# Linear attention feeding a gated MLP on one core: S loaded in two transfers, x scaled tile by tile, and a new order table

## The chip, the cores and the metric

The kernel runs on one core of a Trainium2 chip. The metric is the device time of one execution in microseconds (us). Before the change it was 259.46 us, the median of three runs (258.75, 259.46 and 259.86).

## The reference

The program computes a linear attention and puts its result through a normalised, gated MLP, all in fp32:

```python
def phi(x):                                   # per token: 8 x 8 outer product, 64 features
    a = np.einsum('rd,bhsd->bhsr', S1, x)
    b = np.einsum('rd,bhsd->bhsr', S2, x)
    return np.einsum('bhsi,bhsj->bhsij', a, b).reshape(*x.shape[:-1], r * r)
q_p, k_p = phi(q), phi(k)                     # 4 batches, 4 heads, 1088 tokens, head_dim 32
kv = np.einsum('bhsf,bhsd->bhfd', k_p, v);  z = np.sum(k_p, axis=2)
num = np.einsum('bhsf,bhfd->bhsd', q_p, kv)
den = np.einsum('bhsf,bhf->bhs', q_p, z)[..., None] + 1e-06
x = (num / den), as 4352 tokens x 128
xn = x / sqrt(mean(x * x) + 1e-06) * rms_g
out = (silu(xn @ w_gate) * (xn @ w_val)) @ w_out        # 128 -> 1536 -> 128
```

## The kernel before

**Tiling.** The 4352 tokens are cut into eight chunks of 512 and one of 256. For each of the four batches `kside` computes the key features and the product `kv`; for each chunk `qside` computes the query features, the numerators (L627), the denominators (L645/L646, L649), x (L636), the mean squares `ms` (L655), `rstd` on GpSimd (L668), the scaled rows `xn` (L671 on VectorE or L688 on ScalarE), their transposes on TensorE (L675), and the two parts `x_hi` and `x_lo` (L678, L681) of the MLP's input. The MLP goes by slots: one chunk and one of the 12 blocks of 128 of the 1536 hidden columns. A slot is three matmuls each for the gate and the value (L726: high by high, low weight by high, high weight by low), Silu on ScalarE (L735), the product `h` on VectorE (L738), its high part on ScalarE (L753), its low part on VectorE or GpSimd (L756), and three matmuls into `o_ps` (L764). Weights and S arrive as 64-bit words and are turned into fp32 with bit operations (L346 to L362 for the weights, L371 to L389 for S).

**Start.** S is the small matrix (`sw`, 128 rows of 512 bytes, 64 KB). It lands in `s_raw` and becomes `sblk`, which every first-stage matmul (L485 for keys, L550 for queries) takes as an operand. S is one transfer, the first on ScalarE's DMA queue (L392). The first half of chunk 0 of q follows it on that queue (L524); the other half is on SyncE's queue, behind the first piece of the keys (L457). TensorE runs eight warm-up matmuls on a constant (L337) meanwhile.

**Order.** Nothing is scheduled on the chip: the string `ORDER` lists the numbers of all tasks (1286 of them), and the string `ON` says, for each task that could run on more than one engine, which one has it (a for ScalarE, d for VectorE, p for GpSimd). `Plan.follow` walks the list with a cost for each task and gives each a start; `Plan.run` writes the instructions in the order of these starts. A transfer with a `since` is taken to start at that time; one whose `since` is 0 takes the next place on the common DMA clock. Where the plan sees TensorE idle for long, it puts in further warm-up matmuls.

Of the kernel before, what the change touches and what calls it, by code (L numbers as in the profile page):

```python
# [22 lines left out]
P = 128  # L23
# [61 lines left out]
"""  # L85
ON = (
    "aapddadapaaapaddaaaaaappapdadpapdapdadpadpapdapdaddappappadapadddapaddaaaapdddddaadapapdaaaddddaddddddadpdddddpppdpapdda"
    "paaaadpaaadpddppdppddpaaaddaaapppddpddddppaaadpdddpdpddpddddddadadpdddpdppddppdpdpdaappaaddpppppddpdpddadpddapdpdpddpddd"
    "dadpdddppddpa"
# [15 lines left out]
SLATE = 650  # L105
# [156 lines left out]
def attention_then_glu(ctx, tc, kT, v, qT, sw, w, out):  # L262
# [19 lines left out]
    def on_act(n, emit, sbuf=False, against=0):  # L282
        occ = n * 0.835 + (98 if sbuf else 62)
        return Way(occ, occ + 98, emit, against=against)

    def on_dve(n, emit, lock=False, fast=False, against=0):
        occ = n * (0.52 if fast else 1.04) + 70
        return Way(occ, occ + 82, emit, lock or fast, against)
# [99 lines left out]
    def s_join():  # L388
        nc.vector.tensor_tensor(out=sblk.bitcast(U32), in0=s_tmp.bitcast(U32), in1=s_top, op=ALU.bitwise_or)  # L389

    plan.add({"dma": Way(
        ISSUE + SLATE, P * NB * 8 / 320, lambda: nc.scalar.dma_start(out=s_raw.rearrange("p n c -> p (n c)"), in_=sw.bitcast(U32)), since=740  # L392
    )}, (), ["s_raw"])
# [5 lines left out]
    plan.add({"act": on_act(NB, s_abs, True), "dve": on_dve(NB, s_abs_dve, fast=True)}, ["s_raw", "table"], ["s_tmp"])  # L399
    dve(NB, s_side, ["s_raw"], ["s_top"], fast=True)  # L400
    dve(NB, s_low, ["s_raw", "s_top"], ["s_top"], lock=True)
# [116 lines left out]
    def qload(c):  # L518
        n, s0 = CHUNKS[c], STARTS[c]
        q = qs[c] = sb("q", [P, 512], 2)  # L520
        for i, (lo, hi) in enumerate(((0, n // 2), (n // 2, n)) if not c and QHALVES else ((0, n),)):
            eng = nc.sync if c or i else nc.scalar
            load(
                P * (hi - lo) * 4, lambda eng=eng, lo=lo, hi=hi: eng.dma_start(out=q()[:, lo:hi], in_=qT[:, s0 + lo:s0 + hi]), [(q, i)],  # L524
                since=0 if c or i else 1170,
            )

    def qside(c):
# [133 lines left out]
        for u, wd in ((0, 2), (2, 2)) if first else ((0, nt),):  # L662
# [7 lines left out]
            def scaled(us=us, wd=wd):  # L670
                nc.vector.tensor_tensor(out=xn()[:, us], in0=x()[:, us], in1=rstd()[:, us].to_broadcast([P, wd, DM]), op=ALU.mult)  # L671
# [197 lines left out]
```

## Time and profile before

| | before |
|---|---|
| median of three runs | 259.46 us (258.75 to 259.86) |
| the profiled execution's own time | 258.33 us |
| its span, first to last instruction | 256.5 us |
| TensorE busy | 252.0 us, 98% |
| VectorE / ScalarE / GpSimd busy | 168.6 / 153.8 / 90.6 us |
| granted TensorE clock | 1.00 |

The profiled execution took 1.83 us more than its span, which lies outside the first and last instruction, and it is 1.13 us below the median of the three runs. A row of the timeline gives the start in us from the span's start, the duration, the engine (a "q" behind the name is the engine's instruction queue, which issues DMAs), the line, and the tile written and those read; in brackets stands idle time ahead of it and what ended that. PEld is TensorE's weight load, which runs beside its matmuls. A matmul's duration covers its pipeline, so successive matmuls overlap; the spacing of their starts is what each costs.

### The profile page before, as it was taken

What the parts mean: (1) busy time and instruction counts of PE and PEld (TensorE: products, weight loads), DVE (VectorE), ACT (ScalarE), POOL (GpSimd) and SP (SyncE); (2) the same over time, 40 slices, a digit from 0 to 9 for tenths busy, and PEclk for the clock granted to TensorE, in tenths of its full rate; (3) what the DMA queues carried; (4) which work ended last, traced back from release to release, by engine and by line L of the source; (5) the groups of instructions that cost most, each with busy time, mean ns of one, the idle gap of its engine ahead of it and who ended that gap; (6) DMA issues with size and microseconds to landing.
All of it is one profiled execution on the core that took longest, in us unless ns stands there. A gap on an engine that the chain in (4) does not pass through costs nothing.

```text
span 256.5 us, 5598 instructions
## 1 busy us (share of the span) xinstructions
PE 252.0 (98%) x2116; PEld 204.0 (80%) x2116; DVE 168.6 (66%) x390; ACT 153.8 (60%) x339; POOL 90.6 (35%) x92
## 2 busy tenths in 40 slices
PE   7999999999999999999999999999999999999995
PEld 5888777788887787788887888888888887888895
DVE  2998999989866676646464666647644554635643
ACT  3789888647664744575555555455556655554572
POOL 3444222123755412583516503145223714132031
PEclk9999999999999999999999999999999999999999
DMA  7999886064015115061320120001000100100010
GB/s 236 380 382 279 251 236 208 0 158 130 1 59 149 65 47 139 0 185 43 92 75 3 42 78 15 0 1 43 0 0 0 41 4 0 41 0 3 0 42 20
DMA packets 13498, 22.13 MB, mean 86 GB/s; under 512 B 1952, under 2 KB 5024, under 8 KB 13472
## 3 DMA queue, kind: packets, MB, share of 16 engines
q1 hardware_dynamic: 13040, 21.52, 27.0%
q8 instruction: 16, 0.26, 0.4%
q10 hardware_dynamic: 432, 0.26, 0.3%
q14 instruction: 10, 0.08, 0.1%
HBM read 18.69 MB, written 3.08 MB: 85 GB/s over the span
## 4 chain that ended last, share of the span: by engine, by line
PE 95%; ACT 2%; DMA 1%; POOL 1%; DVE 0%; issue 0%
PE g_ps L726 28%; PE v_ps L726 28%; PE o_ps L764 28%; PE att L627 3%; PE att L497 2%; PE att L675 2%; DMA s_raw<-sw 1%; PE att L485 1%; PE att L578 1%; PE o_ps L497 1%; ACT phiq L309 0%; ACT w_tmp L362 0%; POOL at L439 0%; PE att L745 0%; PE g_ps L485 0%; PE g_ps L558 0%
## 5 line engine op out<-in xcount | busy, mean ns | idle before, releaser
L738 DVE TENSOR_TENSOR h<-v_ps,s 128x512 f32<-128x512 f32 (+2 forms) x110 | 69.9, 649 | 49.7 <-PE v_ps L726 25.7
L756 POOL TENSOR_TENSOR h_lo<-h,h_hi 128x512 fp32r<-128x512 f32 (+1 forms) x43 | 53.0, 1242 | 109.2 <-DVE h_lo L756 39.7
L735 ACT ACTIVATE s<-g_ps 128x512 f32<-128x512 f32 (+1 forms) x108 | 60.8, 574 | 39.8 <-PE g_ps L726 32.7
L753 ACT CAST h_hi<-h 128x512 fp32r<-128x512 f32 (+1 forms) x106 | 61.3, 599 | 38.6 <-DVE h L738 35.5
L756 DVE TENSOR_TENSOR h_lo<-h,h_hi 128x512 fp32r<-128x512 f32 (+1 forms) x63 | 40.8, 660 | 13.4 <-ACT h_hi L753 10.0
L726 PE MATMUL g_ps<-x_hi,w_hi 128*128 128x512 f32 (+1 forms) x110 | 42.5, 387 | 0.0
L726 PE MATMUL v_ps<-x_hi,w_hi 128*128 128x512 f32 (+1 forms) x110 | 42.3, 385 | 0.0
L726 PE MATMUL g_ps<-x_lo,w_hi 128*128 128x512 f32 (+1 forms) x110 | 41.6, 379 | 0.0
L726 PE MATMUL v_ps<-x_hi,w_lo 128*128 128x512 f32 (+1 forms) x110 | 41.6, 378 | 0.0
L726 PE MATMUL g_ps<-x_hi,w_lo 128*128 128x512 f32 (+1 forms) x110 | 41.5, 378 | 0.0
L726 PE MATMUL v_ps<-x_lo,w_hi 128*128 128x512 f32 (+1 forms) x110 | 41.5, 379 | 0.0
L764 PE MATMUL o_ps<-h_hi,w_hi 128*128 128x512 f32 (+1 forms) x106 | 41.3, 389 | 0.0
L764 PE MATMUL o_ps<-h_hi,w_lo 128*128 128x512 f32 (+1 forms) x106 | 40.7, 384 | 0.0
L764 PE MATMUL o_ps<-h_lo,w_hi 128*128 128x512 f32 (+1 forms) x106 | 40.6, 383 | 0.0
L726 PEld LDWEIGHTS g_ps<-x_hi,w_hi 128*128 128x128 f32 x110 | 20.7, 188 | 4.8 <-ACT s L735 0.2
L726 PEld LDWEIGHTS v_ps<-x_hi,w_hi 128*128 128x128 f32 x110 | 20.7, 188 | 4.6 <-DVE h L738 0.3
L726 PEld LDWEIGHTS g_ps<-x_lo,w_hi 128*128 128x128 f32 x110 | 20.7, 188 | 4.2
L726 PEld LDWEIGHTS v_ps<-x_lo,w_hi 128*128 128x128 f32 x110 | 20.6, 188 | 4.2
L726 PEld LDWEIGHTS v_ps<-x_hi,w_lo 128*128 128x128 f32 x110 | 20.7, 188 | 4.0
L726 PEld LDWEIGHTS g_ps<-x_hi,w_lo 128*128 128x128 f32 x110 | 20.7, 188 | 3.9
L764 PEld LDWEIGHTS o_ps<-h_lo,w_hi 128*128 128x128 f32 x106 | 19.9, 188 | 4.3
L764 PEld LDWEIGHTS o_ps<-h_hi,w_hi 128*128 128x128 f32 x106 | 19.9, 188 | 4.1
(97 smaller groups left out, 256.5 us busy)
## 6 DMA issues: line engine op xcount, KB each, us to landing
w_raw<-w SPq DMA_DIRECT2D x12, 384.0 KB
bt<-far SPq DMA_DIRECT2D x24, 128.0 KB
at<-far SPq DMA_DIRECT2D x12, 256.0 KB
outT<-o_sb SPq DMA_DIRECT2D x8, 256.0 KB
q<-qT SPq DMA_DIRECT2D x7, 256.0 KB
vt<-v SPq DMA_DIRECT2D x4, 272.0 KB
kt<-kT SPq DMA_DIRECT2D x4, 256.0 KB
vt<-v SPq DMA_DIRECT2D x3, 340.0 KB
```

The source lines that it names most:

```text
L485: nc.tensor.matmul(out=ab()[n0:rows.stop, (t - lo) * HALF:(t - lo + 1) * HALF], lhsT=kt()[:, s0:s0 + len(rows)], rhs=sblk, start=True, sto ...
L497: nc.tensor.matmul(out=kvv[r0:r0 + wide, h // 2, :], lhsT=phi()[:, t, h * F + f:h * F + f + wide], rhs=vt()[:, t, h, :], start=(t == 0 and ...
L578: nc.tensor.matmul(out=accs[p]()[a * D:(a + 1) * D, :m], lhsT=sab[rows, p].rearrange("p c o r -> p (c o r)"), rhs=q()[rows, a * m:(a + 1) ...
L627: nc.tensor.matmul(out=nv[n0:rows.stop, t, p, :], lhsT=phi()[:, p, l0:l0 + len(rows)], rhs=kvs[cut][:, p, :], start=True, stop=True,)
L675: nc.tensor.transpose(out=xt()[:, t * P:(t + 1) * P], in_=xn()[:, t, :], identity=ident)
L726: nc.tensor.matmul(out=acc()[:, cs], lhsT=wt[:, j, i3, :], rhs=x()[:, cs], start=(i == 0), stop=(i == 2))
L735: act(n, lambda: nc.scalar.activation(out=s()[:, :n], in_=gps()[:, :n], func=AF.Silu), cols(gps, whole[0]), [s])
L738: cs.stop - cs.start, lambda cs=cs: nc.vector.tensor_tensor(out=h()[:, cs], in0=vps()[:, cs], in1=s()[:, cs], op=ALU.mult),
L753: act(n, lambda: nc.scalar.copy(out=h_hi()[:, :n], in_=h()[:, :n]), hs, [h_hi], True)
L756: eng.tensor_tensor(out=h_lo()[:, :n], in0=h()[:, :n], in1=h_hi().bitcast(F32)[:, :n], op=ALU.subtract)
L764: nc.tensor.matmul(out=o_ps()[:, :n], lhsT=wt[:, j, 2, :], rhs=x()[:, :n], start=first and i == 0, stop=last and i == 2,)
```

## The change

Four things change.

- S is loaded in two halves of 64 rows: one on SyncE's queue, one on ScalarE's. Everything that reads `s_raw` waits for both.
- Both halves of q's first chunk are issued from ScalarE's queue.
- On VectorE, x times rstd was one `tensor_tensor` over all tiles of a chunk, with rstd broadcast along the columns. Now it is one `tensor_scalar` for each tile of 128 columns, with one factor per partition.
- `ORDER` and `ON` are new. Since S is now two tasks, all later tasks have numbers that are higher by one.

```diff
 ORDER = """
-1 0 2 3 5 4 10 6 7 18 19 20 14 41 42 43 13 36 11 68 15 37 79 38 22 23 26 30 31 16 24 17 212 32 69 12 27 207 9 208 28 39 80 44 45 8 21 25 29 33 209 213
+1 11 2 0 4 5 3 6 15 7 8 10 19 20 21 14 37 12 69 17 42 43 38 16 80 18 13 23 24 27 44 31 208 39 25 28 29 32 40 209 45 41 33 213 210 70 214 9 81 215 22
...
-SLATE = 650
+SLATE = 250
...
-    plan.add({"dma": Way(
-        ISSUE + SLATE, P * NB * 8 / 320, lambda: nc.scalar.dma_start(out=s_raw.rearrange("p n c -> p (n c)"), in_=sw.bitcast(U32)), since=740
-    )}, (), ["s_raw"])
+    for i, rows in enumerate((slice(0, HALF), slice(HALF, P))):
+        eng = nc.scalar if i else nc.sync
+        plan.add({"dma": Way(ISSUE + SLATE * i, HALF * NB * 8 / 320, lambda eng=eng, rows=rows: eng.dma_start(
+            out=s_raw[rows].rearrange("p n c -> p (n c)"), in_=sw.bitcast(U32)[rows]), since=740 * i)}, (), [("s_raw", i)])
...
-            eng = nc.sync if c or i else nc.scalar
+            eng = nc.sync if c else nc.scalar
...
-                since=0 if c or i else 1170,
+                since=0 if c else 1170 + 430 * i,
...
             def scaled(us=us, wd=wd):
-                nc.vector.tensor_tensor(out=xn()[:, us], in0=x()[:, us], in1=rstd()[:, us].to_broadcast([P, wd, DM]), op=ALU.mult)
+                for t in range(us.start, us.stop):
+                    nc.vector.tensor_scalar(out=xn()[:, t], in0=x()[:, t], scalar1=rstd()[:, t], scalar2=None, op0=ALU.mult)
...
-                "dve": on_dve(wd * P, scaled, True),
+                "dve": Way(wd * 137, wd * 137 + 82, scaled, True),
```

**The first transfers.** These are the first rows of SyncE's queue and then of ScalarE's at the start of the program, before the change. `kt` holds the keys, `q` the queries, `vt` the values, `w_raw` a block of weights, `spare` is a dummy that loads ScalarE's function table.

```order
L457 DMA kt_101<-kT 128x512
L524 DMA q_103<-qT 128x256
L457 DMA kt_101<-kT 128x641
L524 DMA q_108<-qT 128x512
L467 DMA vt_110<-v 128x544
L412 DMA w_raw_112<-w 128x768
...
L392 DMA s_raw<-sw 128x128
L524 DMA q_103<-qT 128x256
L394 ACT_TABLE_LOAD
L394 ACTIVATE spare<-mhalf 128x4
L379 ACTIVATE s_tmp<-s_raw 128x64
```

The same two queues with the change:

```order
L458 DMA kt_101<-kT 128x512
L393 DMA s_raw<-sw 64x128
L458 DMA kt_101<-kT 128x641
L525 DMA q_109<-qT 128x512
L468 DMA vt_111<-v 128x408
L468 DMA vt_111<-v 128x544
...
L393 DMA s_raw<-sw 64x128
L525 DMA q_103<-qT 128x256
L395 ACT_TABLE_LOAD
L395 ACTIVATE spare<-mhalf 128x4
L525 DMA q_103<-qT 128x256
L379 ACTIVATE s_tmp<-s_raw 128x64
```

On ScalarE's queue one half of S is the first transfer. On SyncE's queue the other half is the second, behind the first piece of the keys. The second half of q stands on ScalarE's queue behind the table load and the dummy.

**VectorE's first products.** These are VectorE's rows behind the conversion of S, before the change, and then those around the first reciprocal. `both` is a copy of the two projections, `at` and `phi` are the outer products for queries and keys, `rden` is one over the denominator, `sq` and `ms` belong to the mean square; the 128x768 and 128x512 products are key tiles.

```order
L310 COPY both_143<-att_127 128x128
L439 TENSOR_TENSOR at_152<-att_127,both_143 128x512
L310 COPY both_166<-v_ps_145 128x192
L439 TENSOR_TENSOR phi_141<-v_ps_145,both_166 128x768
L439 TENSOR_TENSOR phi_141<-g_ps_158,both_190 128x768
L310 COPY both_213<-att_176 128x128
L439 TENSOR_TENSOR at_215<-att_176,both_213 128x512
...
L649 RECIPROCAL rden_303<-den_300 128x8
L354 SCALAR_TENSOR_TENSOR w_tmp_274<-w_raw_122,w_tmp_274 128x384
L636 TENSOR_TENSOR x_320<-att_277,rden_303 128x256
L649 RECIPROCAL rden_323<-den_311 128x8
L655 ISA sq_325,ms_326<-x_320 128x128
```

With the change the same places hold:

```order
L310 COPY both_136<-g_ps_128 128x64
L310 COPY both_154<-att_138 128x128
L440 TENSOR_TENSOR at_158<-att_131,both_152 128x512
L440 TENSOR_TENSOR phi_143<-v_ps_145,both_169 128x768
L310 COPY both_194<-g_ps_161 128x192
L440 TENSOR_TENSOR phi_143<-g_ps_161,both_194 128x768
L440 TENSOR_TENSOR phi_143<-v_ps_173,both_191 128x512
L440 TENSOR_TENSOR at_213<-att_206,both_234 128x512
...
L650 RECIPROCAL rden_305<-den_302 128x8
L350 TENSOR_SCALAR w_tmp_277<-w_tmp_277 128x384
L637 TENSOR_TENSOR x_315<-att_279,rden_305 128x256
L650 RECIPROCAL rden_317<-den_313 128x8
```

A key product of 128x512 has come to VectorE from GpSimd, with a copy of 128x64 more and one of 128x128 exchanged for another. Between the first reciprocal and the first x a weight step of another kind stands: L350 in place of L354.

**TensorE around the first MLP matmul.** These rows run from the second numerators of chunk 0 (L627, before) to the first gate matmul (`g_ps<-x_hi`).

```order
L627 MATMUL att_365<-kv_73,phiq_286 64x66 x8
L485 MATMUL v_ps_379<-sblk,kt_132 64x64 x6
L675 MATMUL att_390<-ident,xn_376 128x128 x2
L485 MATMUL g_ps_399<-sblk,kt_132 64x64 x6
L485 MATMUL att_412<-sblk,kt_217 64x64 x6
L726 MATMUL v_ps_425<-x_hi_408,w_hi 128x256
L726 MATMUL v_ps_425<-x_hi_408,w_lo 128x256
```

With the change:

```order
L628 MATMUL att_366<-kv_73,phiq_289 64x66 x8
L677 MATMUL att_383<-ident,xn_375 128x128 x2
L486 MATMUL g_ps_390<-sblk,kt_179 64x64 x6
L486 MATMUL v_ps_404<-sblk,kt_179 64x64 x6
L486 MATMUL att_414<-sblk,kt_211 64x64 x6
L728 MATMUL v_ps_427<-x_hi_398,w_hi 128x256
L728 MATMUL v_ps_427<-x_hi_398,w_lo 128x256
```

One group of six key matmuls has moved from ahead of the first transposes of xn (L675, now L677) to behind them; the number of key matmuls ahead of the first MLP matmul is the same.

More of the change, by code (lines that the diff above doesn't have):

```diff
@@ L48 @@
 ORDER = """
[36 rows of a table removed]
[36 rows of a table added]
 """
 ON = (
-    "aapddadapaaapaddaaaaaappapdadpapdapdadpadpapdapdaddappappadapadddapaddaaaapdddddaadapapdaaaddddaddddddadpdddddpppdpapdda"
-    "paaaadpaaadpddppdppddpaaaddaaapppddpddddppaaadpdddpdpddpddddddadadpdddpdppddppdpdpdaappaaddpppppddpdpddadpddapdpdpddpddd"
-    "dadpdddppddpa"
+    "adpadddadaaadadpaaaaaadpapdadpappaddaddapdappaddadpaddadpadapadadapaadaaaapdpdddaapadadadaaddaaaddddddadpddddpdpddpadada"
+    "paaaapdaaapdddpddddpddaaapdddapdppddpddpdddaapdadapddppdpddppddddpddaddppddpdpppdpdaddpadadpdpdpppddppdaaddddpdddpdppppp"
+    "pappdppddddda"
 )
@@ L397, in s_abs_dve @@
         nc.vector.tensor_scalar(out=s_tmp.bitcast(U32), in0=s_raw[:, :, 1], scalar1=0x7FFFFFFF, scalar2=None, op0=ALU.bitwise_and)
-    plan.add({"act": on_act(NB, s_abs, True), "dve": on_dve(NB, s_abs_dve, fast=True)}, ["s_raw", "table"], ["s_tmp"])
-    dve(NB, s_side, ["s_raw"], ["s_top"], fast=True)
-    dve(NB, s_low, ["s_raw", "s_top"], ["s_top"], lock=True)
+    plan.add({"act": on_act(NB, s_abs, True), "dve": on_dve(NB, s_abs_dve, fast=True)}, [("s_raw", 0), ("s_raw", 1), "table"], ["s_tmp"])
+    dve(NB, s_side, [("s_raw", 0), ("s_raw", 1)], ["s_top"], fast=True)
+    dve(NB, s_low, [("s_raw", 0), ("s_raw", 1), "s_top"], ["s_top"], lock=True)
     dve(NB, s_clamp, ["s_tmp"], ["s_tmp"], fast=True)
```

70 rows, old and new, of the table ORDER are left out of this document.

## The prediction

> **What bounds the kernel now.** I read the profile's page first, then busy times by stretches, then the timeline of the first 24 us, where the change works. The page's head and its first row:
>
> ```profile
> span 256.5 us, 5598 instructions
> PE 252.0 (98%) x2116; PEld 204.0 (80%) x2116; DVE 168.6 (66%) x390; ACT 153.8 (60%) x339; POOL 90.6 (35%) x92
> ```
>
> TensorE is busy for 252.0 of 256.5 us; the other engines are far from it. A shorter program must therefore have fewer or cheaper matmuls, or less of the 4.5 us in which TensorE has none. Where these lie is in the windows view: stretch, its length, busy time of each engine, granted clock, share and rate of the DMA engines.
>
> ```profile
> core 0: us, PE busy (x) PEld busy (x) DVE busy (x) ACT busy (x) POOL busy (x), PEclk, DMA share, GB/s
> 0.00:5.00 5.00, 3.57 (x16) 1.88 (x16) 0.92 (x6) 1.75 (x3) 1.30 (x10) 1.00 0.65 199
> 5.00:11.00 6.00, 5.85 (x149) 5.30 (x150) 4.90 (x10) 3.22 (x12) 3.76 (x4) 1.00 1.02 371
> 11.00:17.60 6.60, 6.37 (x138) 5.01 (x138) 6.07 (x25) 5.92 (x22) 2.91 (x4) 1.00 1.04 403
> 17.60:24.00 6.40, 6.40 (x88) 5.57 (x85) 6.17 (x22) 6.15 (x21) 2.00 (x4) 1.00 0.93 296
> 24.00:236.00 212.00, 212.00 (x1604) 169.64 (x1601) 139.88 (x304) 126.16 (x256) 77.74 (x68) 1.00 0.23 66
> 236.00:256.50 20.50, 17.79 (x131) 16.61 (x129) 10.67 (x28) 10.55 (x28) 2.91 (x4) 1.00 0.06 20
> ```
>
> From 24 to 236 us TensorE is busy for 212.00 of 212.00 us at full clock, with VectorE at 66%. No order of the same matmuls can gain there; it can only lose. What is open is the first 5.0 us, 0.38 us of idle time up to 17.6, and 2.7 us at the end, which hold the last additions and the last store. So the change is worth what it does to the moment of the first real matmul, to the chain behind it up to the first MLP matmul, and to the number of times that TensorE changes tile size. The start, from the timeline:
>
> ```profile
> 0.73 0.41 ACTq L392 DMA_DIRECT2D s_raw<-sw  x1
> ...
> 1.17 0.46 ACTq L524 DMA_DIRECT2D q<-qT  x1
> 1.19 0.41 SPq L524 DMA_DIRECT2D q<-qT  x1
> ...
> 1.65 0.42 SPq L457 DMA_DIRECT2D kt<-kT  x1
> 1.66 1.28 ACT L394 ACT_TABLE_LOAD   x1 [1.66 <-PEq L862]
> ...
> 2.95 0.20 ACT L394 ACTIVATE spare<-mhalf 128x4 f32<-128x4 f32 x1
> ...
> 4.01 0.26 ACT L379 ACTIVATE s_tmp<-s_raw 128x64 f32<-128x64 f32 x1 [0.85 <-DMA s_raw<-sw]
> ...
> 4.76 0.22 DVE L389 TENSOR_TENSOR sblk<-s_tmp,s_top 128x64 uint32<-128x64 uint32 x1
> ...
> 5.04 0.34 PE L485 MATMUL g_ps<-sblk,kt 128*64 128x64 f32 x4 [0.70 <-DVE sblk L389]
> ...
> 5.21 0.64 PE L550 MATMUL att<-sblk,q 128*64 128x64 f32 x16
> ...
> 5.67 0.52 PE L485 MATMUL v_ps<-sblk,kt 128*64 128x64 f32 x12
> ```
>
> The chain of waits opens with the same transfer:
>
> ```profile
> 0.73 3.25 DMA s_raw<-sw
> ```
>
> S is issued at 0.73, has landed at 3.98, is `sblk` at 4.98, and the first real matmul starts at 5.04. Every 0.1 us by which S comes earlier or later moves everything behind it.
>
> **S in two halves.** The change is described as putting S first on both queues. The order says otherwise: on SyncE's queue the first piece of the keys is issued first, and the half of S second, in the place that q's half has now, at 1.19. The other half, on ScalarE's queue, stays at 0.73. Both are waited for, so the later decides. If the second half takes as long from its issue as all of S did, it lands at 1.19 + 3.25 = 4.44, 0.46 later than now. If instead only its size counts, half of S is 32 KB less at the 199 GB/s of the first stretch, 0.16 us, and it lands at 3.82. The bounds are -0.16 and +0.46; I take their middle, +0.15, since the half is small but stands behind 256 KB of keys in its queue. The conversion is the same work as before (six operations, 4.01 to 4.98), so 5.04 becomes 5.19.
>
> The Trainium skill, DMA: Bandwidth & Descriptors, "Issuing engines are not separate DMA queues", says that transfers from several engines run on the same 16 DMA engines, and that issuing from two saves only the issue time. By it two half transfers carry the same bytes behind the same keys, and this term would be 0 and not +0.15; nothing in the trace of before splits a transfer, so no row shows it.
>
> **The second half of q.** It leaves SyncE's queue and is now issued from ScalarE's, behind the table load and the dummy. TensorE needs it in the second half of the row at 5.21: 0.17 us of key matmuls and half of the 0.46 us up to 5.67 put that at 5.44. If ScalarE's queue issues it only when the dummy has ended, at 3.15, it lands at 3.15 + 3.25 = 6.40, 0.96 late. If the queue runs ahead of the engine, it is issued at 1.66 and lands at 4.91, in time. Rows that bear on this, from the view of line 646 and from ScalarE's timeline:
>
> ```profile
> L646 ACTq EVENT_SEMAPHORE  x2: 17/17/17, 15.5 to 16.0; - x2
> ```
>
> ```profile
> 15.48 0.70 ACT L688 ACTIVATE xn<-x,rstd 128x128 f32<-128x128 f32 x2
> 16.08 0.15 ACT L646 ACTIVATE den<-att 128x8 f32<-128x8 f32 x1
> ```
>
> The queue's instruction for line 646 is done at 15.5, when the two scalings of L688 have only begun (15.48 to 16.18). So the queue does run ahead, and I take 0, with +0.96 kept for the range. Behind it nothing new waits: the next ScalarE operation needs S, which is later anyway. On SyncE's queue the key piece at 1.65 keeps its place with less in front, so it comes no later.
>
> The Trainium skill, Perfetto Trace Analysis, "Sequencer Loop", has it that engine instructions are pushed into a queue and the sequencer goes on, but that some instructions are worked on by the sequencer itself. By the first part the term is 0, which agrees with the 15.5 above; if a table load were of the second kind it would be near +0.7 (issue at 2.94), and no row here tells.
>
> **x times rstd.** The rows, first those of the scaling, then two `tensor_scalar` forms that bracket 128 columns (line, engine, operation, tiles, count, busy us and mean ns of one, idle before it):
>
> ```profile
> L671 DVE TENSOR_TENSOR xn<-x,rstd 128x512 f32<-128x512 f32 x3 | 2.0, 672 | 0.2 <-POOL h_lo L756 0.2
> L371 DVE TENSOR_SCALAR s_top<-s_raw 128x64 uint32<-128x64 uint32 x1 | 0.2, 195 | 3.1 <-DMA s_raw<-sw 3.1
> L346 DVE TENSOR_SCALAR w_tmp<-w_tmp 128x384 f32<-128x384 f32 x12 | 4.2, 356 | 0.4 <-POOL at L439 0.2
> ```
>
> Four tiles cost between 4 x 0.195 = 0.78 and 4 x 0.356 = 1.42 us where one operation cost 0.67, so by durations it is +0.1 to +0.75 per chunk, near +0.25 by interpolation to 128 columns; as successive operations overlap, a small gain isn't excluded. In the new order only six tiles are scaled on VectorE (three whole chunks before), the rest on ScalarE. All six lie late, where VectorE has a third of its time free and TensorE always has other matmuls ahead. I take 0; without that cover it would be 0.4 us at most, once for four tiles and once for two.
>
> **The order, first 24 us.** VectorE takes over a 128x512 key product from GpSimd, and a 128x64 copy:
>
> ```profile
> L439 DVE TENSOR_TENSOR at<-att,both 128x512 f32<-128x512 f32 x2 | 1.4, 692 | 0.1
> L439 POOL TENSOR_TENSOR phi<-both 128x512 f32<-128x512 f32 x1 | 1.1, 1072 | 0.0
> ```
>
> The like product costs 0.69 us on VectorE and 1.07 on GpSimd. VectorE's idle time from 5 to 11 us is 6.00 - 4.90 = 1.10 us, which covers 0.69; if it did not, the reciprocals would come up to 0.7 late. Further on, between the first reciprocal and the first x, another step stands:
>
> ```profile
> 12.44 0.36 DVE L350 TENSOR_SCALAR w_tmp<-w_tmp 128x384 uint32<-128x384 uint32 x1
> 12.74 0.20 DVE L649 RECIPROCAL rden<-den 128x8 f32<-128x8 f32 x1
> 12.86 0.54 DVE L354 SCALAR_TENSOR_TENSOR w_tmp<-w_raw,w_tmp 128x384 uint32<-128x384 uint32 x1
> 13.31 0.42 DVE L636 TENSOR_TENSOR x<-att,rden 128x256 f32<-128x256 f32 x1
> ```
>
> Now L354 holds up x by 13.31 - 12.86 = 0.45 us. L350 in its place lasts 0.36 in all, and 0.30 from start to start (12.44 to the reciprocal's start at 12.74). This is the chain x, mean square, rstd, xn, and it ends at xn's end at 16.18, just as TensorE's transposes want it at 16.19. I count the gain at 0.17 us, between 0 and 0.45. The key matmuls that stood ahead of these transposes now stand behind them, equal in number, so they only change sides. TensorE's rows there:
>
> ```profile
> 16.19 0.44 PE L675 MATMUL att<-ident,xn 128*128 128x128 f32 x2
> ...
> 17.60 0.38 PE L726 MATMUL v_ps<-x_hi,w_hi 128*128 128x256 f32 x1
> 17.82 0.28 PE L726 MATMUL v_ps<-x_hi,w_lo 128*128 128x256 f32 x1
> 17.94 0.28 PE L726 MATMUL g_ps<-x_hi,w_hi 128*128 128x256 f32 x1
> ```
>
> **The order, the rest.** The first MLP matmul behind matmuls of another tile size keeps the next one waiting for 0.22 us (17.60 to 17.82), a later one for 0.12: a change of size costs 0.10. Counted in the two orders, there are 30 changes behind the first MLP matmul before and 29 now, so -0.1 us. The matmuls are the same, but for one more warm-up matmul, in the 0.70 us ahead of 5.04 in which TensorE waits; if it ran over, it would cost 0.2 at most. In the last rows the same three groups end the program in the same form, 0, with up to 0.3 either way for a low part that comes late.
>
> **The sum.** +0.15 (S) + 0 (q) + 0 (scaling) - 0.17 (chain to xn) - 0.10 (changes of size) = -0.12 us. The profiled execution took 258.33 us, span 256.5 and 1.83 around it; it becomes 258.2. The median of the runs lies 1.13 above it, so I forecast 259.3 us against 259.46: no change that a measurement can tell, for which I take 0.5%, 1.3 us.
>
> **The rivals.** First, inputs late by their place in the queues: S at its upper bound, q's half behind the dummy. TensorE then reaches that half's matmuls at 6.40 instead of 5.44, and all behind moves by 0.96: 260.3 us. For it speaks the order of ScalarE's rows, against it the queue running ahead at 15.5. It would be slower than before, yet within 0.5%.
>
> Second, new stalls in the long middle, and the result is slower. With TensorE at 212.00 of 212.00 any wait there is a loss. The likeliest is an output product too close behind its gate and value, where the low part has gone to GpSimd:
>
> ```profile
> L756 POOL TENSOR_TENSOR h_lo<-h,h_hi 128x512 fp32r<-128x512 f32 x39 | 50.1, 1294 | 94.1 <-DVE h_lo L756 37.6 <-ACT h_hi L753 20.3 <-PE o_ps L764 8.6
> L756 DVE TENSOR_TENSOR h_lo<-h,h_hi 128x512 fp32r<-128x512 f32 x57 | 38.4, 685 | 12.4 <-ACT h_hi L753 10.0 <-POOL h_lo L756 1.9 <-POOL phi L439 0.4
> ```
>
> Each such case costs 1.29 - 0.69 = 0.61 us; three make 1.8 us and 261.1 us, and it decides from 1.3 us, the third case. Against it: in the new order the distance from a value group to its output product is no shorter than in the old, but for two places in the last 9 us.
>
> Third, faster: the 0.38 us of idle time up to 17.6 go, S comes at its lower bound (-0.16), the chain to xn gains 0.45 and the sizes 0.1, together 1.1: 258.4 us. Only with something at the end as well (0.3) does it pass 1.3.
>
> **How the numbers follow.** The forecast has 0.79, late inputs 0.08, stalls in the middle 0.07, the faster case 0.06. Of the forecast and of late inputs nearly all lies within 0.5%, one in a hundred above it; so faster 0.06, same 0.86, slower 0.08. The range leaves out the stalls: it goes from the faster case, 258.4, to late inputs, 260.3, and 0.3 beyond each, since the runs before alone spread over 1.1 us: 258.1 to 260.6.
>
> **What would show it.** S: the waits on `s_raw` end at 4.0 to 4.3 and the first L486 matmul starts near 5.2; at 5.5 or later the upper bound holds. Q: an issue on ScalarE's queue near 1.7, not 3.0, and no gap of TensorE ahead of the second L551 group. Chain: the first transposes of xn at about 16.2. Middle: TensorE still busy for all of 24 to 236. Scaling: four rows of 0.2 to 0.25 us on L673. The forecast is wrong if TensorE idles behind 24 us, or if the first MLP matmul comes before 16.9 or after 18.6.

## The result and the profile after

The changed kernel takes 260.95 us, the median of seven runs (259.75 to 262.67); the kernel before took 258.75 in the seven runs beside it (258.29 to 259.86). The ratio is 1.009, with a 95% interval of 1.0062 to 1.0117: slower by 0.6 to 1.2%. The profiled execution took 260.80 us, its span is 2.5 us longer than before. Two runs far from all others, 627 us of the kernel before and 351 us of an experiment, are left out of the readings below. The head of its page, with the granted TensorE clock in 40 slices:

```profile
span 259.0 us, 5625 instructions
...
PE 252.7 (98%) x2118; PEld 205.2 (79%) x2118; DVE 171.2 (66%) x398; ACT 152.9 (59%) x345; POOL 87.0 (34%) x87
...
PEclk9799999999999999999999999999999999999999
```

The second digit of the clock is 7; before, no slice was below 9. The windows view by the stretches of the prediction:

```profile
core 0: us, PE busy (x) PEld busy (x) DVE busy (x) ACT busy (x) POOL busy (x), PEclk, DMA share, GB/s
0.00:5.00 5.00, 3.73 (x18) 1.95 (x18) 0.39 (x3) 1.75 (x3) 1.30 (x10) 1.00 0.57 157
5.00:11.00 6.00, 4.27 (x66) 4.02 (x67) 3.62 (x10) 1.53 (x7) 1.69 (x2) 0.72 1.00 364
11.00:17.60 6.60, 6.20 (x158) 5.22 (x156) 5.65 (x20) 5.04 (x15) 1.30 (x2) 1.00 1.02 359
...
24.00:236.00 212.00, 212.00 (x1637) 169.91 (x1635) 145.38 (x317) 126.18 (x270) 70.59 (x62) 1.00 0.24 69
```

The long middle is as full as before, at full clock. Nearly all of the loss lies ahead of 11 us (behind it, up to 17.6 us, TensorE is busy for 6.20 us where it was busy for 6.37): in 5 to 11 us TensorE ran 66 rows where it ran 149, busy for 4.27 us, at a clock of 0.72. In the first 5 us the DMA engines moved 157 GB/s where they moved 199. The start in the timeline:

```profile
0.73 0.39 SPq L458 DMA_DIRECT2D kt<-kT  x1
0.74 0.55 ACTq L393 DMA_DIRECT2D s_raw<-sw  x1
...
1.18 0.59 SPq L393 DMA_DIRECT2D s_raw<-sw  x1
...
1.33 0.60 ACTq L525 DMA_DIRECT2D q<-qT  x1
1.82 0.57 SPq L458 DMA_DIRECT2D kt<-kT  x1
1.95 1.28 ACT L395 ACT_TABLE_LOAD   x1 [1.95 <-issue]
2.02 0.49 ACTq L525 DMA_DIRECT2D q<-qT  x1
...
4.64 0.20 DVE L371 TENSOR_SCALAR s_top<-s_raw 128x64 uint32<-128x64 uint32 x1 [3.77 <-DMA s_raw<-sw]
...
5.74 0.34 PE L486 MATMUL g_ps<-sblk,kt 128*64 128x64 f32 x4 [1.18 <-DVE sblk L389]
...
5.91 0.40 PE L551 MATMUL att<-sblk,q 128*64 128x64 f32 x8
...
7.30 0.69 PE L551 MATMUL att<-sblk,q 128*64 128x64 f32 x8 [0.99 <-DMA q<-qT]
...
7.78 0.85 PE L486 MATMUL v_ps<-sblk,kt 128*64 128x64 f32 x12
```

S's second half holds the conversion up to 4.64 (4.01 before), and the first real matmul starts at 5.74 (5.04). The trace records a transfer's landing in 16 parts: 15 parts of this half of S had landed by 3.94, the last at 4.54. The second half of q is issued at 2.02, ahead of the end of the table load, and yet TensorE waits 0.99 us for it, until 7.30; 14 of its 16 parts had landed by 6.12, the last two at 7.16 and 7.25. Behind it the 12 key rows take 0.85 us where they took 0.52. The first MLP matmul:

```profile
18.67 0.53 PE L677 MATMUL att<-ident,xn 128*128 128x128 f32 x2
20.32 0.39 PE L728 MATMUL v_ps<-x_hi,w_hi 128*128 128x256 f32 x1
```

It starts 2.72 us later than before (17.60). The last matmul of the program ends at 256.13 against 253.78, 2.35 later, so behind the first MLP matmul the new order is 0.37 us shorter.

The clock in the slices around the gap, from the windows view of the changed kernel:

```profile
6.50:7.00 0.50, 0.00 (x0) 0.00 (x0) 0.00 (x0) 0.12 (x1) 0.50 (x1) 1.00 0.97 301
7.00:7.50 0.50, 0.20 (x4) 0.20 (x6) 0.00 (x0) 0.19 (x1) 0.06 (x1) 0.68 0.88 314
7.50:10.50 3.00, 3.00 (x50) 2.88 (x49) 2.27 (x5) 0.85 (x3) 1.07 (x1) 0.50 1.01 388
10.50:11.00 0.50, 0.50 (x6) 0.50 (x5) 0.50 (x1) 0.01 (x1) 0.00 (x0) 0.91 1.06 408
```

0.68 between 7.0 and 7.5 is full clock for 0.18 us and half for the rest; 0.91 between 10.5 and 11.0 is half clock for 0.09. So the clock was halved from 7.18 to 10.59, for 3.41 us, and 7.18 lies in the second of TensorE's two idle times (6.31 to 7.30).

### The profile page after: what moved, and what is told of

It is laid out like the page before. It is cut to its first block, busy times and chain, and to the rows that moved or that the text cites. A ratio compares the mean times of both kernels' runs of the same rounds, so it can differ in the third digit from the quotient of the medians.

```text
span 259.0 us, 5625 instructions
## 1 busy us (share of the span) xinstructions
PE 252.7 (98%) x2118; PEld 205.2 (79%) x2118; DVE 171.2 (66%) x398; ACT 152.9 (59%) x345; POOL 87.0 (34%) x87
## 4 chain that ended last, share of the span: by engine, by line
PE 95%; DMA 2%; ACT 1%; ACTq 0%; DVE 0%; issue 0%
PE v_ps L728 28%; PE g_ps L728 28%; PE o_ps L766 27%; PE att L628 3%; DMA q<-qT 2%; PE att L498 2%; PE att L677 2%; PE att L579 1%; PE att L486 1%; PE o_ps L498 1%; PE g_ps L486 1%; PE att L551 1%; PE v_ps L486 1%; PE att L747 0%; PE g_ps L559 0%; ACTq L525 0%
## 5 line engine op out<-in xcount | busy, mean ns | idle before, releaser
L758 POOL TENSOR_TENSOR h_lo<-h,h_hi 128x512 fp32r<-128x512 f32 (+1 forms) x46 | 57.0, 1247 | 85.9 <-ACT h_hi L755 33.1
L758 DVE TENSOR_TENSOR h_lo<-h,h_hi 128x512 fp32r<-128x512 f32 (+1 forms) x60 | 39.3, 659 | 12.0 <-ACT h_hi L755 5.4
L766 PEld LDWEIGHTS o_ps<-h_hi,w_lo 128*128 128x128 f32 x106 | 19.9, 188 | 4.0
```

Source lines behind the costliest of these rows:

```text
L758: eng.tensor_tensor(out=h_lo()[:, :n], in0=h()[:, :n], in1=h_hi().bitcast(F32)[:, :n], op=ALU.subtract)
L766: nc.tensor.matmul(out=o_ps()[:, :n], lhsT=wt[:, j, 2, :], rhs=x()[:, :n], start=first and i == 0, stop=last and i == 2,)
```

## The experiments

The first theory is loading: the loss comes from where S's half and q's half stand in the queues. Its rival is order: the new table costs it, whatever the loading. Four kernels undo one or both parts of the loading, or make it alone.

**Loading of before, new order and scaling kept (a_sq).**

```diff
-    for i, rows in enumerate((slice(0, HALF), slice(HALF, P))):
-        eng = nc.scalar if i else nc.sync
...
+    for i in range(2):
+        plan.add({"dma": Way(ISSUE + SLATE * i, HALF * NB * 8 / 320, lambda i=i: i and nc.scalar.dma_start(
+            out=s_raw.rearrange("p n c -> p (n c)"), in_=sw.bitcast(U32)), since=740 * i)}, (), [("s_raw", i)])
-            eng = nc.sync if c else nc.scalar
+            eng = nc.sync if c or i else nc.scalar
```

> The changed kernel with the loading of before: S as one transfer on ScalarE's queue, the second half of q on SyncE's queue behind the first keys. New order and scaling by tiles stay. Loading theory (the 2.2 us come from where S and q's second half stand in the queues): first L486 matmul back at 5.0 to 5.1, no gap of TensorE ahead of the second L551 group, first MLP matmul at 17.4 to 17.8, time within 0.3% of the kernel before, 258.2 to 259.3. Order theory (the new order of the first 24 us costs it, whatever the loading): the first L486 matmul is back too, but the first MLP matmul is still at 18.5 or later and the time 260 or more.

Measured 257.96 us (12 runs, 257.64 to 258.90), ratio to before 0.9961 (0.9941 to 0.9982). TensorE's rows:

```profile
5.14 0.34 PE L486 MATMUL g_ps<-sblk,kt 128*64 128x64 f32 x4 [0.15 <-DVE sblk L389]
5.30 0.64 PE L551 MATMUL att<-sblk,q 128*64 128x64 f32 x16
5.77 0.52 PE L486 MATMUL v_ps<-sblk,kt 128*64 128x64 f32 x12
```

No gap, 0.52 for 12 rows, first MLP matmul at 17.52. The order theory falls: with the old loading the new order is not slower than before but 0.2 to 0.6% faster, by more than the loading theory expected.

**The loading of after alone, in the kernel before (b_sq).** Half of S on SyncE's queue behind the first keys, both halves of q on ScalarE's:

```diff
-    nc.scalar.dma_start(out=s_raw.rearrange("p n c -> p (n c)"), in_=sw.bitcast(U32))
+    nc.scalar.dma_start(out=s_raw[HALF:].rearrange("p n c -> p (n c)"), in_=sw.bitcast(U32)[HALF:])
...
     nc.sync.dma_start(out=kt()[:, cs], in_=kT[b][:, cs])
+    nc.sync.dma_start(out=s_raw[:HALF].rearrange("p n c -> p (n c)"), in_=sw.bitcast(U32)[:HALF])
...
-            eng = nc.sync if c or i else nc.scalar
+            eng = nc.sync if c else nc.scalar
```

> The kernel before with the loading of after alone: half of S on SyncE's queue behind the first keys, both halves of q on ScalarE's queue; old order, old scaling. Loading theory: first L485 matmul at 5.7, a gap ahead of the second half of q's matmuls of 1 us or more, time 260.3 to 261.3, as slow as the changed kernel or slower. Order theory: 258.3 to 259.2, as the kernel before.

Measured 262.10 us (6 runs), ratio 1.0124 (1.0091 to 1.0156). The time is 0.8 us above the range of the loading theory, and the first L485 matmul comes at 4.96 and not at 5.7: S was in time, and the wait is for q alone:

```profile
7.33 1.04 PE L550 MATMUL att<-sblk,q 128*64 128x64 f32 x16 [2.04 <-DMA q<-qT]
```

So the loading costs 262.10 - 258.93 = 3.2 us in the old order, against the kernel before beside it, and 260.95 - 257.96 = 3.0 in the new one.

**S split, q's half back on SyncE (a_q).** The edit is the one of `eng` for q in the diff of a_sq, alone.

> The changed kernel with q's second half back on SyncE's queue, between the half of S and the second keys; S stays split. Loading theory, q part: the half of q lands before 6.0, the gap of 0.99 us ahead of the second L551 group goes, and with it the lower clock; what stays is S's 0.7 us: first L486 at 5.7, first MLP matmul near 18.4, 259.2 to 259.8. If S's split alone makes the whole loss (all inputs late together): 260.5 or more. Order theory: 260.5 or more as well, but with TensorE's losses behind 8 us.

Measured 259.02 us (258.80 without the one far run), ratio 1.0001 (0.9978 to 1.0025): 0.8 to 1.1 above a_sq, under the range expected.

```profile
5.49 0.48 PE L486 MATMUL g_ps<-sblk,kt 128*64 128x64 f32 x4 [0.50 <-DVE sblk L389]
5.76 1.07 PE L551 MATMUL att<-sblk,q 128*64 128x64 f32 x16
6.62 0.85 PE L486 MATMUL v_ps<-sblk,kt 128*64 128x64 f32 x12
```

S came at 4.39, and there is no gap ahead of q's second half, as expected. But the rows run at half speed (0.85 us for 12 where a_sq has 0.52), of which the theory said nothing, and the first MLP matmul comes at 19.46 and not near 18.4. The eleven other runs fall into two groups, 258.28 to 258.80 and 259.25 to 259.92, and the profiled one is of the upper; so the 0.8 to 1.1 are not the price of the split alone.

**S whole, both halves of q on ScalarE (a_s).** The edit is the one of S in the diff of a_sq, alone.

> The changed kernel with S as one transfer on ScalarE's queue; both halves of q stay on that queue. Loading theory: first L486 at 5.0 to 5.1. If q's half is late because of the queue in which it stands (third there, issued near 2.0 and last to be served), it lands at 6.5 to 7.2 all the same, TensorE waits 1.2 to 1.8 us for it, and the time is 260.0 to 260.9. If it was late because the half of S had been put ahead of it and the keys, it lands by 5.6, there is no gap, and the time is 258.2 to 259.2. Order theory: 260 or more with no gap there.

Measured 258.78 us, ratio 0.9993 (0.997 to 1.0015): 0.8 above a_sq. Issue and arrival:

```profile
1.72 0.39 ACTq L525 DMA_DIRECT2D q<-qT  x1
...
6.65 0.45 PE L551 MATMUL att<-sblk,q 128*64 128x64 f32 x8 [1.06 <-DMA q<-qT]
```

The gap is there, as the queue-place theory had it, but the time is 1.2 us under its range: the wait is shorter than the 1.2 to 1.8 expected, and in this trace the clock stayed up. (Of the twelve runs only the slowest, 260.41 us, has a mean granted clock of 0.993, as the changed kernel's profiled run has.) S split (0.8 to 1.1) and q moved (0.8) make less together than the 3.0 of both. One part of what is missing is in the DMA engines. One window, 3.5 to 4.5 us, of a_s, then of a_q, then of the changed kernel:

```profile
3.50:4.50 1.00, 0.94 (x5) 0.34 (x4) 0.59 (x4) 0.26 (x1) 0.00 (x0) 1.00 1.10 396
```

```profile
3.50:4.50 1.00, 0.94 (x5) 0.34 (x4) 0.11 (x1) 0.12 (x1) 0.00 (x0) 1.00 0.61 184
```

```profile
3.50:4.50 1.00, 0.94 (x6) 0.33 (x4) 0.00 (x0) 0.00 (x0) 0.00 (x0) 1.00 0.73 203
```

With S whole the engines are busy throughout at 396 GB/s; with S split they have too little to do, just then. The rows of issue fit that: with the half of S in the queues most of the first issues take 0.49 to 0.60 us (0.41 to 0.46 before), and there is one more, so the issue of the second keys ends at 1.82 + 0.57 = 2.39, where a_s has issued both pieces of the keys by 1.60. It does not account for all of the distance from 6.65 (S whole) to 7.3 (S split): the bulk of q's half lands 0.22 us later (14 parts by 6.12, against 15 by 5.90), and the rest is the last parts (7.16 and 7.25, against 6.61). In all five traces with S split and q on ScalarE's queue the last part lands between 7.18 and 7.28, also where the parts come evenly (b_sq, from 5.58 to 7.20). What sets that time stays open.

**The clock.** The other part of what is missing is the clock. Of 28 runs of the kernel before beside these, 15 took 258.2 to 258.9 us and 13 took 259.5 to 260.2: two groups, while a_sq has one. The new order has one warm-up matmul more, so in a_sq TensorE was idle for 0.15 us ahead of the first real matmul, where the kernel before has 0.70. A second theory: TensorE's clock is decided by how idle it was, and half clock costs about as much as the groups are apart. Nine warm-up matmuls in the kernel before (b_w):

```diff
-WARM = 8
+WARM = 9
```

> The kernel before with nine warm-up matmuls in place of eight, nothing else. Clock theory: the runs of the kernel before fall in two groups (258.2 to 258.9 and 259.5 to 260.2) since TensorE, idle for 0.7 us ahead of the first real matmul, starts the first real matmuls at half clock in some runs; with that idle time filled the upper group goes: all runs in 258.2 to 258.9, median 258.3 to 258.5. Rival (the two groups come from when inputs land, not from the clock): both groups stay, median 258.3 to 260.

Measured 258.34 us, all 12 runs from 258.14 to 258.90, ratio 0.9973 (0.9953 to 0.9994); the kernel before beside it had its two groups again. So the clock theory's forecast came true and the rival's did not. Yet the profiled run doesn't show the idle time filled: TensorE waits 0.77 us in it, since the clock went up at 3.52 already and the last warm-up matmuls took half the time. What the ninth does is read from the twelve times, not from this trace. The reverse, a_sq without its further warm-up matmul (a_sqw; the filler of the plan emits nothing):

```diff
-    PLAN = plan, plan.run({...}, keep_warm, ...)
+    PLAN = plan, plan.run({...}, lambda k, n, s: None, ...)
```

> The changed kernel with the loading of before, and without the one further warm-up matmul that the new order has. Clock theory: the idle time of 0.7 us ahead of the first real matmul is back, and with it the two groups of times: some runs at 257.6 to 258.3, others 1.2 to 1.8 us above, as in the kernel before. If the further warm-up matmul does nothing and the order gains by itself: all runs in 257.6 to 258.9, as with it.

Measured 259.12 us: five runs from 257.69 to 258.49, seven from 259.02 to 259.63. As expected, two groups. The profiled run is one of the upper group:

```profile
5.00 0.48 PE L486 MATMUL g_ps<-sblk,kt 128*64 128x64 f32 x4 [0.66 <-DVE sblk L389]
5.27 1.07 PE L551 MATMUL att<-sblk,q 128*64 128x64 f32 x16
6.12 0.85 PE L486 MATMUL v_ps<-sblk,kt 128*64 128x64 f32 x12
```

S is no later than in a_sq, but 12 rows take 0.85 us against 0.52; the first MLP matmul is at 18.68, 1.16 later.

**The changed kernel with its gaps filled.** Three more warm-up matmuls ahead of S and four ahead of the second half of q's matmuls (a_w), then five in the second gap alone (a_w2, the last two lines; a_w has a 4 in place of the 5):

```diff
-    PLAN = plan, plan.run({...}, keep_warm, ...)
+    PLAN = plan, plan.run({...}, lambda k, n, s: keep_warm(k + 3, n, s), ...)
...
                 def abmm(u=u, ab=ab):
+                    first and u == 2 and keep_warm(5, "att", 2)
                     for t in range(2):
```

> The changed kernel with seven more warm-up matmuls: three ahead of S, four in the gap ahead of the second half of q's matmuls. No input comes earlier. Clock theory: the two waits stay (0.7 and about 1 us), but the rows of L486 behind them stand 29 and not 54 ns apart, and 0.8 to 1.5 us come back: 259.2 to 260.1. Waiting theory (the loss is the late inputs alone): 260.7 to 261.3, as the changed kernel.

Measured 261.05 us (6 runs), ratio 1.0079 (1.0049 to 1.011): the time that the waiting theory forecast, and not the clock theory's. The trace has the clock at full from 4.03 on, but S came earlier too in it (first L486 at 5.29), the first MLP matmul is at 19.64 and the span 258.3, 0.7 less than the changed kernel's. The time did not follow: it lies 1.9 to 2.8 us above the span, where the kernels above have 1.7 to 1.9. Why isn't known, so this run decides neither way.

> The changed kernel with five warm-up matmuls in the second gap only, ahead of the second half of q's matmuls; the first gap stays. No input comes earlier, and fewer are added than in the run before, whose span fell by 0.7 us while its time did not. Clock theory: L486 behind the gap at 29 ns from row to row, first MLP matmul 0.6 us or more ahead of the 20.3 of the changed kernel, span 258.0 to 258.5, time 259.8 to 260.4. Waiting theory (only the late inputs count): first MLP matmul at 20.3, 260.8 to 261.3. If it is the time outside the span that grows with further warm-up matmuls: span 258.4, but time minus span above 1.9 again and time 260.8 or more.

Measured 260.44 us (260.01 to 261.89), ratio to before 1.0075 (1.0051 to 1.0099).

```profile
5.95 1.27 PE L337 MATMUL att<-const-float32-0.0 128*1 128x128 f32 x10
...
7.23 0.45 PE L552 MATMUL att<-sblk,q 128*64 128x64 f32 x8
7.51 0.52 PE L486 MATMUL v_ps<-sblk,kt 128*64 128x64 f32 x12
```

q's half came no earlier (7.23), but the 12 rows are back at 0.52 and the first MLP matmul at 19.34. From q's second half on that is 19.34 - 7.23 = 12.11 us, against 20.32 - 7.30 = 13.02: the half clock costs 0.9 us of span. The span came out where the clock theory had it (258.0), the time at the upper end or just above, with time outside the span again longer in some runs (1.75 to 2.34). So the 0.9 us rest on two traces; by their times alone a_w2 and the changed kernel can't be told apart (1.0051 to 1.0099 against 1.0062 to 1.0117). The single runs bear it out in part. Of the 13 runs of the changed kernel (with the six of after2 below) eight have a mean granted clock of 0.993, which is what one halved step of 3.41 us makes of 259 us, and took 260.79 to 261.77 us. Of the five at 1.00 one is the fastest, 259.75, but four are the slowest, 261.85 to 262.67; no trace of these four exists, and why they are slow isn't known.

**What makes q's half late (a_kq).** S whole, and q's second half third on SyncE's queue, behind the second keys, instead of third on ScalarE's:

```diff
     nc.sync.dma_start(out=kt()[:, cs], in_=kT[b][:, cs])
+    first and i and nc.sync.dma_start(out=qs[0]()[:, 256:], in_=qT[:, 256:512])
...
-    eng.dma_start(out=q()[:, lo:hi], in_=qT[:, s0 + lo:s0 + hi])
+    i or eng.dma_start(out=q()[:, lo:hi], in_=qT[:, s0 + lo:s0 + hi])
```

> The changed kernel with S as one transfer on ScalarE's queue and q's second half on SyncE's queue, but behind the second keys: third there, as it was third on ScalarE's queue, issued near 1.65. Line theory (all transfers share the 16 DMA engines, and what counts is the bytes issued ahead): it lands as late as from ScalarE's queue, 6.0 to 6.7, TensorE waits 0.6 to 1.1 us for it, and the time is 258.4 to 259.2. Queue theory (ScalarE's queue is served later than SyncE's): it lands by 5.5, no gap, 257.6 to 258.2.

Measured 258.01 us, ratio 0.9966 (0.9946 to 0.9986). Issued at 1.65, as late as in a_s, it is in time:

```profile
1.65 0.42 SPq L458 DMA_DIRECT2D q<-qT  x1
...
5.25 0.70 PE L551 MATMUL att<-sblk,q 128*64 128x64 f32 x16
```

So it isn't being third that makes it late, and the queue theory's forecast came true. One reading of it: on ScalarE's queue it runs beside what SyncE's queue issues in the same moment (in a_s chunk 1's q, 256 KB, at 1.65); on SyncE's those bytes stand behind it. In a_s 15 of its 16 parts have landed by 5.90 and one at 6.61, in a_kq all by 5.29. 256 KB at the 396 GB/s above are 0.65 us, an estimate that is near the distance from 5.29 to 5.90. No run moves those bytes alone, so this reading is argued and not shown, and what held up the last part stays open.

**S in fact first on both queues (a_s1).** The half of S ahead of the first keys, q's half on SyncE, no further warm-up matmul:

```diff
+    first and not i and nc.sync.dma_start(out=s_raw[:HALF].rearrange("p n c -> p (n c)"), in_=sw.bitcast(U32)[:HALF])
     nc.sync.dma_start(out=kt()[:, cs], in_=kT[b][:, cs])
```

> The changed kernel with the half of S in fact first on SyncE's queue, ahead of the first keys, the other half first on ScalarE's; q's second half third on SyncE's queue, ahead of the second keys; without the further warm-up matmul, which would stand in the way of an earlier S. Line theory: with 256 KB of keys no longer ahead of it S lands at 3.2 to 3.7 and the first keys a little later than before, first L486 matmul at 4.4 to 4.8, time 257.3 to 257.9 where the clock is up by then. If splitting itself makes S late (two issues, more packets): S at 3.9 or later as in the changed kernel, first L486 at 5.0 or later, 258 to 259.5.

Measured 259.28 us (258.43 to 260.36), ratio 1.0002 (0.9978 to 1.0026): not faster.

```profile
3.41 0.20 DVE L371 TENSOR_SCALAR s_top<-s_raw 128x64 uint32<-128x64 uint32 x1 [2.55 <-DMA s_raw<-sw]
...
5.19 0.34 PE L486 MATMUL g_ps<-sblk,kt 128*64 128x64 f32 x4 [1.10 <-DMA kt<-kT]
```

S comes 0.6 earlier, as the line theory had it, but the first matmul needs the keys as well, and these now come last, so neither theory's account held. The profiled run is one of the two slowest of the twelve, the only two with a mean granted clock of 0.993 (260.28 and 260.36 us).

**The scaling (a_sqx).** a_sq with the old broadcast product:

```diff
-                for t in range(us.start, us.stop):
-                    nc.vector.tensor_scalar(out=xn()[:, t], in0=x()[:, t], scalar1=rstd()[:, t], scalar2=None, op0=ALU.mult)
+                nc.vector.tensor_tensor(
+                    out=xn()[:, us], in0=x()[:, us], in1=rstd()[:, us].to_broadcast([P, wd, DM]), op=ALU.mult)
```

> The changed kernel with the loading of before and the old scaling: x times rstd as one tensor_tensor of all tiles with rstd broadcast, new order kept. My term for the scaling was 0: 257.8 to 258.2, within 0.1% of the same kernel with the scaling by tiles. If scaling by tiles carries the gain of the new version: 258.5 or more; if it costs: 257.6 or less.

Measured 257.86 us, ratio 0.9958 (0.994 to 0.9975), against 257.96 by tiles: no difference.

**The changed kernel once more (after2).**

> The changed kernel itself once more, for a second trace and times on the same chip as the two others. All theories: 259.8 to 262.7, median near 261. If the half of S behind the keys lands anywhere from 3.9 to 4.7 by chance, its first L486 matmul differs from the 5.74 of the first trace; q's half lands at 7.2 to 7.4 again, with a gap of TensorE ahead of it whose length is 7.3 less the end of the first half's matmuls.

Measured 261.31 us, ratio 1.0093 (1.006 to 1.0125).

```profile
5.11 0.34 PE L486 MATMUL g_ps<-sblk,kt 128*64 128x64 f32 x4 [0.49 <-DVE sblk L389]
...
7.33 0.69 PE L551 MATMUL att<-sblk,q 128*64 128x64 f32 x8 [1.66 <-DMA q<-qT]
7.81 0.85 PE L486 MATMUL v_ps<-sblk,kt 128*64 128x64 f32 x12
```

This time S's halves were in time, 0.63 earlier than in the first trace, and it gained nothing: q's half came at 7.33 all the same. The first MLP matmul is at 20.37, as in the first trace. S's delay was hidden behind q's.

## Why the prediction was wrong

It forecast 259.3 us with a range up to 260.6, no change; the kernel is slower by 2.2 us. Point by point:

**S.** Forecast +0.15, bounds -0.16 and +0.46. Split with the keys ahead, S's conversion could begin at 4.64, 4.01, 4.39, 4.07, 4.34 and 3.94 in six traces (changed kernel twice, a_q, a_w, a_w2, b_sq), against 3.84 to 4.04 in seven traces with S whole: between nothing and +0.6, so my upper bound was a little too low; in the first trace it is the last of 16 parts that is late. Not the step that failed: after2 shows that this delay did not set the time. By the Trainium skill (DMA: Bandwidth & Descriptors, "Issuing engines are not separate DMA queues") the term was 0, which after2 agrees with and the first trace does not.

**The second half of q: the step that failed.** "If the queue runs ahead of the engine, it is issued at 1.66 and lands at 4.91, in time", and "I take 0, with +0.96 kept". The first part was right, an issue at 2.02 and not 3.0. The landing was wrong: I gave it S's 3.25 us from issue, a duration of a transfer that is first in its queue with idle DMA engines. It took 7.30 - 2.02 = 5.3, beyond even the upper bound of 6.40. The need was at 5.44, so the term is +1.86, not 0. Of this 0.7 is the bulk (14 of 16 parts by 6.12), the rest the last two parts. That its place in the queues makes it late is shown by a_sq, b_sq and a_kq; what makes the last parts late is not. "Behind it nothing new waits" was right for ScalarE and beside the point.

**The clock: a term that was missing.** I read a granted clock of 1.00 in all stretches as a constant, and the 0.70 us ahead of the first matmul as idle time that costs only itself. With 2.05 us idle between 3.76 and 7.18 the clock was halved for 3.41 us, +0.9. The sum at the first MLP matmul is then 1.86 + 0.9 - 0.2 for the chain to xn, near the 2.72 measured. The clock also stands behind the 1.13 us that the sum adds as if they were fixed: the profiled execution (258.33) is of the lower group of the kernel before, the median of three (259.46) at the edge of the upper.

**Chain to xn.** Forecast -0.17. From the reciprocal to x it is 0.35 us now (15.64 to 15.99), 0.57 before: -0.22. Right; and in a_sq, with no late input, it is 12.38 us from the first real matmul to the first MLP matmul, where it was 12.56: -0.18.

**Scaling.** Forecast 0, and a_sqx agrees; but the rows cost 281 ns each, above the 0.20 to 0.25 that I gave:

```profile
L673 DVE TENSOR_SCALAR xn<-x,rstd x6: 278/281/281, 168.9 to 215.7; 128x128 f32<-128x128 f32 x6
```

**The order, the rest.** Forecast -0.10; behind the first MLP matmul it is -0.37, and no single row that I know of carries it. **The further warm-up matmul** I priced at 0 to +0.2: it is worth a gain, since it does away with the upper group of times. Together they make a_sq 0.4% faster than before. **Stalls in the middle:** none, as forecast.

The rival "inputs late" (260.3, at 0.08) was right that inputs come late by their place in the queues, but by a route that did not occur: q's half issued behind the dummy, where it was issued at 2.02. It was priced by S's duration as well, and left out the clock; that 260.3 lies near 260.95 is in part luck.

## What to carry to other kernels

A transfer's duration from issue holds for its place: a row of the first transfer is no price for a moved load. The bytes that all queues issue ahead of it and beside it, and the issues that push back the rest, are a better start by a_s and a_kq, though the last parts came up to 1.1 us behind the rest here. Idle time of TensorE near the start has a second price, the clock of the next microseconds; short fillers in the gaps are worth a try, and a kernel whose times fall in two groups can be a sign of it. Of the three parts of this change the new order with its warm-up matmul is worth keeping (257.96 us), the scaling is neutral, and the loading is not.

## What the runs showed of the hardware

The clock records of the traces change only in steps of 3.413 us, at moments that differ from run to run: full clock lasts 74, 73 or 75 such steps to the end, the halved stretch one. Counting TensorE's idle time in the step before each decision (idle times under 0.1 us left out):

| trace | step, us | idle in it, us | clock behind it |
|---|---|---|---|
| before | 1.05 to 4.46 | 0.12 | goes to full |
| b_w | 0.10 to 3.52 | 0.67, ahead of its first matmul | goes to full |
| a_q | 3.20 to 6.62 | 0.50 | not yet full |
| a_sqw | 2.13 to 5.55 | 0.66 | not yet full |
| b_w | 3.52 to 6.93 | 0.77 | stays full |
| a_w2 | 3.88 to 7.29 | 0.83 | stays full |
| a_s | 4.20 to 7.61 | 0.17 + 1.06 | stays full |
| a_s1 | 3.69 to 7.11 | 1.10 + 0.75 | halved |
| changed | 3.76 to 7.18 | 1.18 + 0.87 | halved |
| after2 | 3.87 to 7.29 | 0.49 + 1.62 | halved |
| b_sq | 4.06 to 7.47 | 0.69 + 2.04 | halved |

To stay up, 1.23 us of idle time in 3.41 was not too much, and 1.85 was. For going up no such figure comes out: the clock did not go up after 0.50 (a_q) and 0.66 (a_sqw), and did after 0.67 (b_w), so idle time alone does not decide it. Steps that lie ahead of a trace's first record are counted back from that record, which is of full clock (4.46 before, 3.52 in b_w, 10.03 in a_q, 8.96 in a_sqw); in b_w the first matmul starts at 0.77. The Trainium skill (TensorE: Matmul & The Clock Gate, "Part 1: The HAM clock gate") has a free-running window of 3413 ns, which agrees with the steps. The same page of the Trainium skill, "Why this matters for your kernels", advises against idle gaps above some 3 us; by these runs 1.85 us of idle time in two gaps was enough, and the measurement decides. Ahead of the first record the profile shows the clock as 1.00 while rows run at half speed (0.85 us for 12 rows in a_sqw): the rows tell, not the column.
